# One activation table, k normalised before its transpose, and a merged low-rank product in an attention and mixer kernel

## The chip, the cores and the metric

The kernel runs on one core of one Trainium2 chip. The core's engines are TensorE (PE; its weight loads are listed apart as PEld), VectorE (DVE), ScalarE (ACT), GpSimd (POOL) and SyncE (SP). Each takes its own instructions strictly in order of its queue, and semaphores hold an instruction until what it needs is done. The metric is the device time of one launch in microseconds.

## The reference

Eight batches, each with twelve heads of 448 rows and 64 columns. First cosine attention: q and k are divided by their norms, the scores divided by tau = 0.1, then softmax, then the product with v. The heads' outputs side by side form `x` of 448 x 768 per batch. Then a mixer: a low-rank mix along the sequence, added to `x`, and a two-layer network along the channels with a residual.

```python
q_n = q / (norm(q) + 1e-06);  k_n = k / (norm(k) + 1e-06)
attn = softmax(q_n @ k_n.T / tau)
x = heads_side_by_side(attn @ v)              # (8, 448, 768)
u = x + (x.T @ U @ V).T                       # U (448, 32), V (32, 448)
out = u + relu(u @ w_ch1) @ w_ch2             # w_ch1 (768, 3072), w_ch2 (3072, 768)
```

## The kernel before, in words

The sequence of 448 is cut into four parts of 112 rows (row = 4 s + c, for c = 0 to 3), which lie on 112 partitions. Heads are taken two at a time: a batch has six pairs, 48 pairs in all. Everything is computed in bf16 with fp32 sums in PSUM.

`attention_pair` (from L92) does one pair. POOL issues six DMAs (L101, L105, L109: two each for q, k and v, with a cast from fp32 to bf16 on the way) and then writes a column of ones behind v (L112), from which the sums of the softmax come. The three tiles come from pools with six buffers, so the q load of pair n has to wait until pair n-6 is done with its q, and likewise for k and v. DVE squares q and k and sums each row (L118 to L121, eight sums each). ScalarE then takes `Ln` of the sixteen sums (L124) and computes the inverse norms as `Exp(-0.5 * ln)`, once for q with ln(1/tau) as the bias (L125) and once for k (L127). DVE multiplies q by its inverse norm (L131). TensorE transposes q and k in eight small matmuls against the identity (L138, L143); DVE copies q's transpose out (`qT`, L149) and k's twice, each time with one head's rows masked to zero (`kTz`, L151, L153). For each head and each of four parts of k, TensorE makes 112 x 448 scores (L160) and ScalarE takes their exponential (L166); k's inverse norm comes in there, as a scale operand with one value per partition. With the exponentials as weights, TensorE makes `av_ps` in 16 matmuls per head (L178), and DVE divides by the sums (L185, L187) into `X_sb`. No maximum is subtracted.

The mixer of a batch runs while the attention of the next batch runs, in seven pieces. Piece 0 starts with `moe_stage0` (L190): TensorE transposes `X_sb` (L199, 24 matmuls) and DVE copies it out (L204); TensorE makes A = U^T x in eight matmuls of 384 columns (L210) and ScalarE copies it out (L216); TensorE makes h from A and V in six matmuls of 448 columns (L221), and DVE adds h and the transposed x into `uT_all` (L227). Pieces 0 to 3 are the first layer, `moe_mlp1`: 24 groups of six matmuls (L235), each ending in a relu on ScalarE (L241). Pieces 4 and 5 are the second layer, `moe_mlp2`: six groups of 24 matmuls (L248), each ending in an add on DVE (L254). The last piece, `moe_store`, transposes the result back (L264), copies it out on ScalarE (L270) and stores it through SP's queue. After the last batch's attention its mixer runs alone.

The weights of the two layers come in 30 DMAs (L89), issued by POOL among the first batch's loads. The order of each engine's queue is not the order of the text: a scheduler of the framework orders the instructions by costs that it assumes, and puts in the semaphores. In what it made, ScalarE takes the `Ln` of pair n after the exponentials of pair n-6 (from pair 13 on), and in the first batch just after those of pair n-1. It also puts in the loads of ScalarE's function table where the next function isn't in the table that is loaded.

The PSUM tags are `ps_tp` (all transposes, two buffers), `ps_sc` (scores, two), `ps_av` (two) and `ps_mlp` (stage 0 and both layers, two).

Of the kernel before, what the change touches and what calls it, by code (L numbers as in the profile page):

```python
# [9 lines left out]
FP = mybir.dt.float32  # L10
# [6 lines left out]
def kernel(  # L17
# [26 lines left out]
    ln_inv_tau = math.log(inv_tau)  # L44
# [6 lines left out]

    ident = const.tile([128, 128], BF, name="ident")
    make_identity(nc, ident)

    b_lt = const.tile([128, 1], FP, name="b_lt")
    nc.gpsimd.memset(b_lt, ln_inv_tau)
# [14 lines left out]

    V_sb = const.tile([128, SCH, SC], BF, name="V_sb")
    nc.gpsimd.memset(V_sb, 0.0)
    nc.gpsimd.dma_start(out=V_sb[0:R], in_=moe_V.rearrange("r (s c) -> r s c", c=SC))

# [6 lines left out]
    for nch in range(NC):  # L82
        weight_dmas.append((w2_sb[:, nch, :], moe_w_ch2[nch * 128:(nch + 1) * 128, :]))
# [7 lines left out]
    emit_weight_dmas.done = 0  # L91

    def attention_pair(b, p, X_sb):
# [14 lines left out]
        for hh in range(2):  # L108
# [15 lines left out]
        nc.scalar.activation(lnq2, q2k2, AF.Ln)  # L124
        nc.scalar.activation(inv_qk[:, :, :, 0], lnq2[:, :, :, 0], AF.Exp,  # L125
                             bias=b_lt[0:SCH, :], scale=-0.5)
        nc.scalar.activation(inv_qk[:, :, :, 1], lnq2[:, :, :, 1], AF.Exp,  # L127
                             bias=b_zero[0:SCH, :], scale=-0.5)

        qn_pair = attnp.tile([SCH, SC, 2, D], BF, name="qn_pair", tag="qn_pair")  # L130
        nc.vector.tensor_mul(  # L131
            qn_pair, q_pair,
            inv_qk[:, :, :, 0:1].to_broadcast([SCH, SC, 2, D]))
# [3 lines left out]
        for c in range(SC):  # L137
            nc.tensor.transpose(  # L138
                out=qkT_ps[:, c, :],
                in_=qn_pair[:, c, :, :],  # L140
                identity=ident[:SCH, :SCH],
            )
            nc.tensor.transpose(  # L143
                out=qkT_ps[:, SC + c, :],
                in_=k_pair[:, c, :, :],
                identity=ident[:SCH, :SCH],
            )
# [9 lines left out]
        for hh in range(2):  # L157
            for jc in range(SC):
                sc_ps = psum.tile([SCH, S], FP, name="sc_ps", tag="ps_sc", bufs=2)
                nc.tensor.matmul(  # L160
                    out=sc_ps,
                    lhsT=kTz[:, hh, jc, :],
                    rhs=qT.rearrange("p a b -> p (a b)"),
                    start=True, stop=True,
                )
                nc.scalar.activation(  # L166
                    out=attn_uT[:, hh, jc, :],
                    in_=sc_ps,
                    func=AF.Exp,
                    scale=inv_qk[:, jc, hh, 1:2],  # L170
                )

        for hh in range(2):
# [18 lines left out]
    def moe_stage0(b, X_sb):  # L192

        XT_all = batchp.tile([128, CC, S], BF, name="XT_all", tag="XT_all")
        for cc in range(CC):
            xt_ps = psum.tile([128, SC, SCH], BF, name="xt_ps", tag="ps_tp",
                              bufs=2)
            for sb in range(SC):
                nc.tensor.transpose(  # L199
                    out=xt_ps[:, sb, :],  # L200
                    in_=X_sb[:, sb, cc * 128:(cc + 1) * 128],
                    identity=ident[:SCH, :SCH],
                )
            nc.vector.tensor_copy(out=XT_all[:, cc, :], in_=xt_ps)  # L204

        A_sb = batchp.tile([128, 2, C // 2], BF, name="A_sb", tag="A_sb", bufs=1)
        for half in range(2):
            a_ps = psum.tile([128, 512], FP, name="a_ps", tag="ps_mlp", bufs=2)
            for sb in range(SC):
                nc.tensor.matmul(  # L210
                    out=a_ps[:, 0:C // 2],
                    lhsT=U_sb[:, sb, :],
                    rhs=X_sb[:, sb, half * (C // 2):(half + 1) * (C // 2)],
                    start=(sb == 0), stop=(sb == SC - 1),
                )
            nc.scalar.copy(out=A_sb[:, half, :], in_=a_ps[:, 0:C // 2])  # L216

        uT_all = batchp.tile([128, CC, S], BF, name="uT_all", tag="uT_all")
        for cc in range(CC):
            h_ps = psum.tile([128, S], FP, name="h_ps", tag="ps_mlp", bufs=2)  # L220
            nc.tensor.matmul(  # L221
                out=h_ps,
                lhsT=A_sb.rearrange("p a b -> p (a b)")[:, cc * 128:(cc + 1) * 128],
                rhs=V_sb.rearrange("r s c -> r c s"),
                start=True, stop=True,
            )
            nc.vector.tensor_add(out=uT_all[:, cc, :], in0=h_ps,  # L227
                                 in1=XT_all[:, cc, :])
        return uT_all

    def moe_mlp1(uT_all, relu1, nchs):
        for nch in nchs:
            m1_ps = psum.tile([128, S], FP, name="m1_ps", tag="ps_mlp", bufs=2)
            for cc in range(CC):
                nc.tensor.matmul(  # L235
                    out=m1_ps,
                    lhsT=w1_sb[:, cc, nch * 128:(nch + 1) * 128],
# [3 lines left out]
            nc.scalar.activation(out=relu1[:, nch, :], in_=m1_ps, func=AF.Relu)  # L241

    def moe_mlp2(uT_all, relu1, ccs):
        outT = uT_all
        for cc in ccs:
            m2_ps = psum.tile([128, S], FP, name="m2_ps", tag="ps_mlp", bufs=2)
            for nch in range(NC):
                nc.tensor.matmul(  # L248
                    out=m2_ps,
                    lhsT=w2_sb[:, nch, cc * 128:(cc + 1) * 128],  # L250
                    rhs=relu1[:, nch, :],
                    start=(nch == 0), stop=(nch == NC - 1),
                )
# [21 lines left out]
    def _split(n, k):  # L275
        base, rem = divmod(n, k)
        res, start = [], 0
        for i in range(k):
# [74 lines left out]
```

## Time and profile before

| what | value |
|---|---|
| median of 5 runs | 818.09 us (817.6 to 819.26) |
| the profiled execution | 822.62 us, of which its span is 820.8 |
| granted TensorE clock, mean | 0.989 |
| PE busy | 717.7 us (87%), 5104 matmuls |
| ACT busy | 494.8 us (60%) |
| DVE busy | 307.1 us (37%) |
| POOL busy | 226.6 us (28%) |
| q, k and v loads: time to issue, and median from issue to landing | 0.70 us each; 2.8, 2.8 and 2.9 us |

A group in the profile is one line's instructions on one engine: its busy time, the mean of one in nanoseconds, then how long the engine was idle just before such an instruction and what ended the wait. The end of a matmul is modelled and matmuls overlap, so PE's busy time says little of how fully it is used; the distance between the starts of matmuls that follow each other says more. The chain is found by going back from the last instruction, at each step to what released it. "issue" is time in which an engine waited for nothing that the profile shows.

### The profile page before, as it was taken

Reading aid. Unit: us, or ns where it says so; the run is one execution under the profiler, and the core shown is the slowest. Engines: PE = TensorE matmul, PEld = TensorE weight load, DVE = VectorE, ACT = ScalarE, POOL = GpSimd, SP = SyncE. Lnnn points to the kernel's source line nnn. Section 1 sums busy time; section 2 is a strip of 40 time slices with the busy share of each in tenths; the row PEclk is TensorE's granted clock in tenths of the full one; section 3 lists DMA queues with packets and bytes.
Section 4 is the critical chain, followed back from the end, with each engine's and each line's share of the span. In section 5 each row is a group of like instructions: output and inputs, shape, how many; then the busy total and the mean of one; then the engine's idle time right before and its main releaser. Section 6 shows DMA issues by size and latency. Waiting matters only on the chain.

```text
span 820.8 us, 12706 instructions
## 1 busy us (share of the span) xinstructions
PE 717.7 (87%) x5104; PEld 427.2 (52%) x5104; DVE 307.1 (37%) x720; ACT 494.8 (60%) x862; POOL 226.6 (28%) x382
## 2 busy tenths in 40 slices
PE   3456777999889989899979998899979999999996
PEld 2344544555455555556545555455545556654553
DVE  2253673434433362444424362344523351123000
ACT  3467688944785478844777369755778357622411
POOL 6477932321323232221423231422322100000000
PEclk9999999999999999999999999999999999999999
DMA  8999952524524262424524261434342120002002
GB/s 122 188 140 144 76 37 18 36 18 85 34 18 30 22 91 20 27 19 85 34 18 29 18 97 12 31 21 86 24 29 18 12 68 1 2 1 68 1 0 68
DMA packets 142618, 37.84 MB, mean 46 GB/s; under 512 B 135104, under 2 KB 138208, under 8 KB 142560
## 3 DMA queue, kind: packets, MB, share of 16 engines
q0 software_dynamic: 138464, 26.03, 38.6%
q1 hardware_dynamic: 4096, 11.01, 4.2%
q8 instruction: 40, 0.66, 0.3%
q14 instruction: 18, 0.15, 0.1%
HBM read 52.02 MB, written 11.01 MB: 77 GB/s over the span
## 4 chain that ended last, share of the span: by engine, by line
PE 62%; ACT 18%; issue 7%; DMA 6%; DVE 3%; POOL 3%; DVEq 0%; POOLq 0%; ACTq 0%
PE m_ps L248 25%; PE m_ps L235 16%; PE sc_ps L160 9%; PE av_ps L178 6%; ACT L124 4%; ACT attn_uT L166 4%; ACT L166 3%; DMA q_pair<-in_q_dram 3%; ACT relu L241 3%; DMA v_pair<-in_v_dram 2%; PE o_ps L264 1%; PE h_ps L221 1%; PE a_ps L210 1%; ACT O_sb L270 1%; POOL v_pair L109 1%
## 5 line engine op out<-in xcount | busy, mean ns | idle before, releaser
L166 ACT ACTIVATE attn_uT<-sc_ps,inv_qk 112x448 bf16<-112x448 f32 x384 | 221.2, 633 | 105.2 <-PE sc_ps L160 101.9
L235 PE MATMUL m_ps<-uT_all,w_sb 128*128 128x448 bf16 x1152 | 251.7, 357 | 10.3 <-ACT relu L241 9.7
L248 PE MATMUL m_ps<-relu,w_sb 128*128 128x448 bf16 x1152 | 234.6, 352 | 0.0
L160 PE MATMUL sc_ps<-qT,kTz 128*112 128x448 bf16 x384 | 141.9, 391 | 43.1 <-ACT attn_uT L166 26.2
L178 PEld LDWEIGHTS <-attn_uT 112*112 112x112 bf16 x1536 | 124.9, 141 | 81.2 <-issue 32.2
L235 PEld LDWEIGHTS <-w_sb 128*128 128x128 bf16 x1152 | 107.3, 99 | 106.4 <-issue 24.3
L248 PEld LDWEIGHTS <-w_sb 128*128 128x128 bf16 x1152 | 107.7, 98 | 91.6
L241 ACT ACTIVATE relu<-m_ps 128x448 bf16<-128x448 f32 x192 | 101.0, 539 | 89.4 <-PE m_ps L235 89.3
L178 PE MATMUL av_ps<-v_pair,attn_uT 112*112 112x65 bf16 x1536 | 145.4, 221 | 3.2 <-ACT attn_uT L166 3.2
L109 POOL DMA_DIRECT2D v_pair<-in_v_dram x96 | 67.1, 703 | 272.6 <-issue 263.5
L105 POOL DMA_DIRECT2D k_pair<-in_k_dram x96 | 67.0, 703 | 98.6 <-PE qkT_ps L143 83.8
L270 ACT CAST O_sb<-o_ps 112x768 f32<-112x768 bf16 x32 | 23.2, 808 | 100.4 <-PE o_ps L264 100.4
L160 PEld LDWEIGHTS <-kTz 128*112 128x112 bf16 x384 | 52.5, 143 | 44.0 <-DVE kTz L151 26.5
L254 DVE TENSOR_TENSOR uT_all<-m_ps,uT_all 128x448 bf16<-128x448 f32 x48 | 29.9, 623 | 120.5 <-PE m_ps L248 120.5
L101 POOL DMA_DIRECT2D q_pair<-in_q_dram x96 | 67.3, 706 | 8.5 <-DVE qn_pair L131 3.5
L118 DVE TENSOR_TENSOR sq_tmp<-q_pair 112x512 bf16<-112x512 bf16 x48 | 20.3, 423 | 114.3 <-DMA q_pair<-in_q_dram 114.1
L185 DVE RECIPROCAL rd<-av_ps 112x4 f32<-112x4 f32 x96 | 17.2, 179 | 119.3 <-PE av_ps L178 118.9
L124 ACT ACT_TABLE_LOAD x47 | 60.3, 1283 | 1.8 <-PEq L334 0.7
L138 PE MATMUL qkT_ps<-ident,qn_pair 112*128 112x112 bf16 x192 | 27.6, 225 | 37.0 <-DVE qn_pair L131 35.8
L131 DVE TENSOR_TENSOR qn_pair<-q_pair,inv_qk 112x512 bf16<-112x512 bf16 x48 | 33.1, 689 | 43.3 <-ACT inv_qk L125 43.2
L166 ACT ACT_TABLE_LOAD x37 | 47.5, 1283 | 0.7
L187 DVE TENSOR_TENSOR X_sb<-av_ps,rd 112x256 bf16<-112x256 f32 x96 | 40.6, 423 | 2.6
(42 smaller groups left out, 457.5 us busy)
## 6 DMA issues: line engine op xcount, KB each, us to landing
out_dram<-O_sb SPq DMA_DIRECT2D x32, 336.0 KB, 3.6
q_pair<-in_q_dram POOLq DMA_DIRECT2D x96, 56.0 KB, 2.8
k_pair<-in_k_dram POOLq DMA_DIRECT2D x96, 56.0 KB, 2.8
v_pair<-in_v_dram POOLq DMA_DIRECT2D x96, 56.0 KB, 2.9
w_sb<-in_moe_w_ch_dram POOLq DMA_DIRECT2D x6, 768.0 KB, 8.6
w_sb<-in_moe_w_ch_dram POOLq DMA_DIRECT2D x24, 192.0 KB, 6.0
U_sb<-in_moe_U_dram POOLq DMA_DIRECT2D x1, 28.0 KB, 2.5
V_sb<-in_moe_V_dram POOLq DMA_DIRECT2D x1, 28.0 KB, 2.6
```

The source lines that it names most:

```text
L101: nc.gpsimd.dma_start(out=q_pair[:, :, hh, :], in_=q[b, h0 + hh].rearrange("(s c) d -> s c d", c=SC))
L105: nc.gpsimd.dma_start(out=k_pair[:, :, hh, :], in_=k[b, h0 + hh].rearrange("(s c) d -> s c d", c=SC))
L109: nc.gpsimd.dma_start(out=v_pair[:, :, hh, 0:D], in_=v[b, h0 + hh].rearrange("(s c) d -> s c d", c=SC))
L124: nc.scalar.activation(lnq2, q2k2, AF.Ln)
L131: nc.vector.tensor_mul(qn_pair, q_pair, inv_qk[:, :, :, 0:1].to_broadcast([SCH, SC, 2, D]))
L160: nc.tensor.matmul(out=sc_ps, lhsT=kTz[:, hh, jc, :], rhs=qT.rearrange("p a b -> p (a b)"), start=True, stop=True,)
L166: nc.scalar.activation(out=attn_uT[:, hh, jc, :], in_=sc_ps, func=AF.Exp, scale=inv_qk[:, jc, hh, 1:2],)
L178: nc.tensor.matmul(out=av_ps[:, ic, 0:D + 1], lhsT=attn_uT[:, hh, jc, ic * SCH:(ic + 1) * SCH], rhs=v_pair[:, jc, hh, :], start=(jc == 0), ...
L187: nc.vector.tensor_mul(X_sb[:, :, c0:c0 + D], av_ps[:, :, 0:D], rd.to_broadcast([SCH, SC, D]))
L235: nc.tensor.matmul(out=m1_ps, lhsT=w1_sb[:, cc, nch * 128:(nch + 1) * 128], rhs=uT_all[:, cc, :], start=(cc == 0), stop=(cc == CC - 1),)
L241: nc.scalar.activation(out=relu1[:, nch, :], in_=m1_ps, func=AF.Relu)
L248: nc.tensor.matmul(out=m2_ps, lhsT=w2_sb[:, nch, cc * 128:(cc + 1) * 128], rhs=relu1[:, nch, :], start=(nch == 0), stop=(nch == NC - 1),)
```

## The change

Five things change.

1. The table set `natural_log_exp_and_others` is loaded once, ahead of everything else.
2. k is multiplied by its inverse norm on DVE before its transpose (`kn_pair`), and 1/tau goes into the product for q (`scalar_tensor_tensor`). One `Exp` on ScalarE gives both inverse norms, and the exponentials of the scores have no scale operand.
3. The matrix M = I + U V is computed once at the start, in bf16 (`M_sb`), from a transposed U and an identity whose columns are in V's order (`ident_int`). Stage 0 is then x^T M in one step: for each of the six parts of the channels, four matmuls of 448 columns into `u_ps`, and one DVE copy. The transposes of x, A, and h are gone.
4. The `Ln` of pair n is tied to come, in ScalarE's order, after the last exponential of an earlier pair: pair n-1 up to n = 6, then a distance that grows to five pairs. The tie is one of order on the same engine and has no semaphore.
5. Names of loop variables change (`nch` to `ncb`, `k` to `parts`).

The scheduler orders all queues anew.

```diff
-    ln_inv_tau = math.log(inv_tau)
...
+    nc.scalar.preload_act_table_set("natural_log_exp_and_others")
     ident = const.tile([128, 128], BF, name="ident")
     make_identity(nc, ident)
-    b_lt = const.tile([128, 1], FP, name="b_lt")
-    nc.gpsimd.memset(b_lt, ln_inv_tau)
...
+    ident_int = const.tile([SCH, SC, S], BF, name="ident_int")
+    nc.gpsimd.memset(ident_int, 0.0)
+    for cs in range(SC):
+        make_identity(nc, ident_int[:, cs, cs * SCH:(cs + 1) * SCH], nomemset=True)
+
+    uT_ps = psum.tile([128, SC, SCH], BF, name="uT_ps", tag="ps_tp", bufs=2)
+    for cs in range(SC):
+        nc.tensor.transpose(
+            out=uT_ps[:, cs, :],
+            in_=U_sb[:, cs, :],
+            identity=ident[:SCH, :SCH],
+        )
+    U_T = const.tile([128, SC, SCH], BF, name="U_T")
+    nc.vector.tensor_copy(out=U_T, in_=uT_ps)
+
+    M_sb = const.tile([SCH, SC, S], BF, name="M_sb")
+    for cs in range(SC):
+        m_ps = psum.tile([SCH, S], FP, name="m_ps", tag="ps_mlp", bufs=2)
+        nc.tensor.matmul(
+            out=m_ps,
+            lhsT=U_T[:, cs, :],
+            rhs=V_sb.rearrange("r s c -> r c s"),
+            start=True, stop=True,
+        )
+        nc.vector.tensor_add(out=M_sb[:, cs, :], in0=m_ps,
+                             in1=ident_int[:, cs, :])
...
+    last_exp = {}
...
-        nc.scalar.activation(lnq2, q2k2, AF.Ln)
-        nc.scalar.activation(inv_qk[:, :, :, 0], lnq2[:, :, :, 0], AF.Exp,
-                             bias=b_lt[0:SCH, :], scale=-0.5)
-        nc.scalar.activation(inv_qk[:, :, :, 1], lnq2[:, :, :, 1], AF.Exp,
+        ln_i = nc.scalar.activation(lnq2, q2k2, AF.Ln)
+        n = b * NPAIR + p
+        if n > 0:
+            gate = n - 1 if n <= 6 else max(6 + (n - 7) // 2, n - 5)
+            tc.add_manual_dep(
+                ln_i.ins, last_exp[gate].name,
+                mybir.DependencyInfo(mybir.DependencyClass.NoSync,
+                                     mybir.DependencyReason.DATA),
+                reason="Ln after the last exponential of an earlier pair")
+        nc.scalar.activation(inv_qk, lnq2, AF.Exp,
                              bias=b_zero[0:SCH, :], scale=-0.5)
...
+        nc.vector.scalar_tensor_tensor(
+            out=qn_pair, in0=q_pair, scalar=inv_tau,
+            in1=inv_qk[:, :, :, 0:1].to_broadcast([SCH, SC, 2, D]),
+            op0=ALU.mult, op1=ALU.mult)
+        kn_pair = attnp.tile([SCH, SC, 2, D], BF, name="kn_pair", tag="kn_pair")
         nc.vector.tensor_mul(
-            qn_pair, q_pair,
-            inv_qk[:, :, :, 0:1].to_broadcast([SCH, SC, 2, D]))
+            kn_pair, k_pair,
+            inv_qk[:, :, :, 1:2].to_broadcast([SCH, SC, 2, D]))
...
-                in_=k_pair[:, c, :, :],
+                in_=kn_pair[:, c, :, :],
...
-                nc.scalar.activation(
+                e_i = nc.scalar.activation(
                     out=attn_uT[:, hh, jc, :],
                     in_=sc_ps,
                     func=AF.Exp,
-                    scale=inv_qk[:, jc, hh, 1:2],
-                )
-
+                )
+
+        last_exp[n] = e_i.ins
...
     def moe_stage0(b, X_sb):
...
         uT_all = batchp.tile([128, CC, S], BF, name="uT_all", tag="uT_all")
         for cc in range(CC):
+            u_ps = psum.tile([128, S], FP, name="u_ps", tag="ps_mlp", bufs=2)
+            for cs in range(SC):
+                nc.tensor.matmul(
+                    out=u_ps,
+                    lhsT=X_sb[:, cs, cc * 128:(cc + 1) * 128],
+                    rhs=M_sb[:, cs, :],
+                    start=(cs == 0), stop=(cs == SC - 1),
+                )
+            nc.vector.tensor_copy(out=uT_all[:, cc, :], in_=u_ps)
         return uT_all
```

## The prediction

> **What bounds the kernel now.** I read the page's busy shares first, then the groups by line, then a table of stretches cut where the first mlp1 matmul of each batch starts (105.46, 204.93, 297.02 ... 755.47), and last the chain and ScalarE's timeline inside one stretch.
>
> The groups (busy, mean ns of one, then the idle time before them):
>
> ```profile
> L166 ACT ACTIVATE attn_uT<-sc_ps,inv_qk 112x448 bf16<-112x448 f32 x384 | 221.2, 633 | 105.2 <-PE sc_ps L160 101.9
> ...
> L241 ACT ACTIVATE relu<-m_ps 128x448 bf16<-128x448 f32 x192 | 101.0, 539 | 89.4 <-PE m_ps L235 89.3
> ...
> L124 ACT ACT_TABLE_LOAD x47 | 60.3, 1283 | 1.8 <-PEq L334 0.7
> ...
> L131 DVE TENSOR_TENSOR qn_pair<-q_pair,inv_qk 112x512 bf16<-112x512 bf16 x48 | 33.1, 689 | 43.3 <-ACT inv_qk L125 43.2
> L166 ACT ACT_TABLE_LOAD x37 | 47.5, 1283 | 0.7
> ```
>
> With ten more loads at L125, ScalarE reloads its table 94 times, 120.6 us, because Ln and Exp alternate. Is that on the path? The stretches (us, busy PE, PEld, DVE, ACT, POOL, granted clock, DMA share, GB/s):
>
> ```profile
> 0.00:105.46 105.46, 58.43 (x382) 41.89 (x383) 44.27 (x106) 60.21 (x99) 75.19 (x136) 1.00 1.18 132
> 105.46:204.93 99.47, 88.34 (x647) 51.89 (x647) 46.98 (x109) 71.17 (x122) 28.07 (x46) 0.98 0.41 38
> ...
> 485.33:578.30 92.97, 85.75 (x640) 50.99 (x638) 38.66 (x91) 61.58 (x108) 25.92 (x43) 1.00 0.40 38
> ...
> 673.01:755.47 82.46, 80.94 (x575) 46.88 (x573) 22.33 (x58) 39.09 (x74) 0.00 (x0) 1.00 0.06 18
> 755.47:820.80 65.33, 58.17 (x312) 30.27 (x311) 4.23 (x7) 15.98 (x28) 0.00 (x0) 0.94 0.07 22
> ```
>
> The last full stretch (673 on) has no loads and no DMA from POOL: PE idles 1.5 us in it, in a middle batch 7.2. But it holds one attention pair less (575 records against 640), so 82.5 is no target yet. The chain inside the middle batch says what stops PE (start, us, what):
>
> ```profile
> 489.34 1.28 ACT L124
> ...
> 493.23 1.28 ACT L166
> ...
> 500.32 1.28 ACT L124
> ...
> 504.74 8.35 issue
> ...
> 514.49 0.69 POOL q_pair L101
> 515.18 3.61 DMA q_pair<-in_q_dram
> 518.88 0.44 DVE sq_tmp L118
> ...
> 520.81 0.58 PE sc_ps L160 x2
> ...
> 527.04 1.28 ACT L124
> ...
> 530.93 1.28 ACT L166
> ...
> 570.30 1.28 ACT L166
> ```
>
> Two causes: loads that hold back a relu or the first exponential; and a q load that POOL issues only after the v load ahead of it (which waits for an old pair's av), while DVE's in-order queue has this q's square ahead of the present pair's qT and kTz. Otherwise PE is the bound.
>
> PE's own work in one batch, from start-to-start times: mlp1 and mlp2 288 x 0.189 (55 in 10.41 us) = 54.4; scores 48 x 0.189 = 9.1; av 192 x 0.058 (13 in 0.76) = 11.2; q/k transposes 48 x 0.05 = 2.4; output transposes 24 x 0.053 = 1.3; stage 0: X transposes 24 x 0.05 = 1.2, A 8 x 0.163 = 1.3, h 6 x 0.19 = 1.15. Sum 82.1 of 92.97: 10.9 us of gaps.
>
> **The change, part by part.**
> *Table set preloaded.* The instruction order that both programs are built to shows 94 loads before and one after, at the start. ScalarE loses 93 x 1.283 = 119.3 us. The Trainium skill ("ScalarE: Activation LUTs", What ACT_TABLE_LOAD costs) prices each switch at 1283 ns plus a 1380 ns drain, 2.66 us; that would make 247 us. ScalarE's timeline (start, us, operation) has no drain between the load and what follows:
>
> ```profile
> 77.98 1.28 ACT L124 ACT_TABLE_LOAD   x1
> 79.27 0.21 ACT L124 ACTIVATE lnq<-q2k 112x16 f32<-112x16 f32 x1
> 79.50 1.28 ACT L125 ACT_TABLE_LOAD   x1
> ```
>
> So I take the row, 1.28. In a middle batch the loads (two a pair) are worth only what they keep PE waiting, and that lies in the 10.9 us of gaps; in the first batch, where each pair waits for the one before, the two of a pair lie on the path whole: 2.57 us.
>
> *Exponentials without a scale operand.* L166 takes 633 ns, the relu of the same length, without pointer operands, 539. The trace can't say whether the 94 ns are Exp's or the operand's; the same section of that page gives each pointer operand about 93 ns and every function the same rate. I take 540: 384 x 0.093 = 36 us of ScalarE. If the page did not hold here it is 0. In a middle batch a pair's eight exponentials take 4.56 us (7 x 0.56 + 0.63); consecutive scores share two PSUM buffers, so the pitch falls by about half of the 93 ns: 4.15. This matters because the new PE order puts fewer mlp matmuls among the scores (m2 pairs: 9 where there were 12; m1: 8 to 11 where there were 11 to 15). Work from the first score to the last av group in an m2 pair: 8 x 0.189 + 9 x 0.189 + 19 x 0.058 = 4.3, against 0.5 + 4.15 = 4.65 of ScalarE: 0.3 to 0.4 idle a pair, as now (5.1 against 4.9). At 633 ns it would be 0.8.
>
> *k normalised on DVE.* One more 112x512 product, nearest row L131, 0.69: 33 us of DVE, which is 37% busy. The qn product becomes a two-operator form with no row: between L118's 0.42 and two passes of L131, 1.38; I take 0.69, as the fp32 broadcast is the same. In the steady state both stand three pairs ahead of use and cost nothing; in the first batch, where pair waits for pair, kn adds its 0.6 pitch. The two small Exps (0.30 + 0.19 pitch) become one.
>
> *Stage 0.* PE loses 3.65 (above) and gains 24 x 0.189 = 4.54: +0.9. ScalarE loses the A copies (7.2 us in all), DVE six XT copies at 0.385 per batch; six adds become six copies, 0.62. The boundary loses its serial path (A copy, then h paced by DVE's adds at 0.61): PE's stretch from o_ps to mlp1 was 284.15 to 296.84, 12.7 us. Now work there is 1.3 + 4.5 + 3.4 (one pair) + 1.2 = 10.4, and 0.5 to 1 idle while O_sb copies (4 x 0.73) free the transposes' buffer.
>
> *Ln gate and order.* In the new order Ln of pair n stands after the exponentials of pair n-5 (before, n-6), and its Exp right behind it; q's square stands ahead of the present pair's reciprocal rather than ahead of the next pair's qT. But POOL's queue now has the ones-memset (which waits for v's landing) ahead of the q issue. Counted from an av's end: v issues 1.4, lands 2.6, q issues 1.4, lands 2.8, so the square can go at +8.3; the reciprocal behind it is wanted at about +8.4. PE needs nothing from it until the next pair's qT, two pairs on. I price this at 0; uncovered it is the third rival.
>
> *Preparing M.* Ahead of the first q issue POOL gets a memset of 1792 columns (535 ns for 512: 1.9) and four selects (0.29 each): +3.1 us, and all DMA with it. PE's queue opens with U's four transposes and four matmuls, DVE's with a copy and four adds (0.62 each) that wait for V: behind them stands pair 0 alone, whose first square goes at about 11.6, not 7.46. Pairs 1 and 2 wait for DMA anyway, so of these 4 us only the 3.1 of the DMA remain.
>
> **The sum**, by stretch.
> *Until the first mlp1 matmul, 105.5 now.* Pairs 0 to 2 are timed by DMA (the square of pair 1 waits until 27.2): +3.1. From pair 2 on the period is 12.2 (exponentials end at 53.5, 65.8, 78.0, 90.1). New: Ln and Exp 0.6, qn to kTz to score 3.85 + 0.6, exponentials 5.2: about 10. But DVE's new order has the square of pair 5 ahead of pair 3's reciprocals and of pair 7 ahead of pair 5's qT; q7 was issued at 76.9, is now at 80, lands at 83.5. So pair 5 ends near 91, and pair 6 needs q9 (94). Ln to kn 2, transposes and kTz 2, the last u copy: first mlp1 matmul at 97. The shorter period alone, with no wait for these loads, would put it at about 90.
> *First batch with mlp, 99.5.* POOL runs at 4.7 us a pair to catch up and the squares of pairs 12, 14 and 16 hold DVE; about 7 us of stalls: 92.
> *Five middle batches, 468.1.* 82.1 + 0.9 = 82.9 work, 5 x 0.35 idle, 0.5 in the boundary: 85 each, 425.
> *Last full one, 82.5.* Its work is 82.9 less one pair (8 x 0.189 + 32 x 0.058 + 24 x 0.05 = 4.6), 78.3; idle 2.2 (1.5 as now, and the wait for the last u copy): 80.5. By the same count the present one has 77.5 of work and 5 of gaps, 4.1 of them in its stage 0. *Tail,* unchanged, 65.3.
> Together 97 + 92 + 425 + 80.5 + 65.3 = 759.8 of span. The profiled execution took 822.62 for a span of 820.8, and the median of the runs is 818.09, 2.7 under the span: **757 us**.
>
> **Rivals.**
> *A, PE tight from the start (15%).* POOL's early waits shrink as the pairs get faster: first matmul at 90, then 86, 5 x 83.3, 79, 65: 737, median 734. For it: POOL's waits between 40 and 70 us are short (0.3 to 0.8). Against: the DMA share of that stretch is 1.18.
> *B, ScalarE still paces the pairs (12%).* Exp stays at 633: 0.5 more for 42 pairs, 21 us: 778. For it: no Exp without the operand in the trace.
> *C, the square holds DVE (15%).* Landing of q reaches 4.6 at the most after 200 us; 1 us over on each of some 24 m1 pairs: 781.
> *D, slower (3%).* The same queue closes into a loop: av end, v 4.0, q 4.2, square and reduction 1.1, then reciprocals, kTz, scores and av of the pair after next, about 9: 18.5 us in two pairs, which PE needs 21 for. It decides above 21; to lose all of 61 us over 28 m1 pairs, 2.2 us each, both landings would have to be near 6: 830.
> *E, not as it says (1%).* Loads could return or the set be left out: 818. The built order has one load.
>
> **How the numbers follow.** The first forecast has 54%, with its own range of 745 to 769. 735 to 781 leaves out half of A and half of C, D and E, some 2 in 10. Within 0.2% of 818.09 (1.6 us; about what these runs can tell from no change) is only E, 1%; faster 96%, slower 3%.
>
> **What would show it.** One load row; L166's successor near 540; PE's idle in a middle batch near 2 to 3; no chain piece of a q load before a score; the first mlp1 matmul near 97; batches of 85. Wrong if the reciprocals wait for squares, if exponentials stay at 633, or if u_ps waits for DVE's copies.

## The result and the profile after

The median is 753.78 us (752.04 to 755.15) against 818.74 us for the kernel before in the same comparison: a ratio of 0.9205, 95% interval 0.9192 to 0.9218. One of the nine executions was slow, 765.33 us with a granted clock of 0.952, and stands outside this range and the ratio. The forecast was 757, its own range 745 to 769. The profiled execution took 753.76 us, its span is 751.9 us.

The page of the kernel after: busy shares, the chain's shares by engine, and three groups (busy, mean ns of one, idle before and what ended it).

```profile
PE 705.9 (94%) x5000; PEld 420.2 (56%) x5000; DVE 316.5 (42%) x725; ACT 331.7 (44%) x705; POOL 229.4 (31%) x386
...
PE 87%; DMA 7%; POOL 3%; ACT 1%; issue 1%; DVE 1%; POOLq 0%; DVEq 0%; ACTq 0%
...
L203 ACT ACTIVATE attn_uT<-sc_ps 112x448 bf16<-112x448 f32 x384 | 191.7, 544 | 160.2 <-PE sc_ps L197 157.2
...
L253 ACT ACTIVATE relu<-m_ps 128x448 bf16<-128x448 f32 x192 | 104.2, 543 | 115.3 <-PE m_ps L247 115.3
```

The exponentials now take what a relu takes, 544 ns. ScalarE fell from 494.8 to 331.7 us, and nearly all its waits are waits for TensorE. 87% of the chain is PE. Two groups of the full list of the same kernel: one table load is left of 94, and the new product for k takes 682 ns, with DVE never idle before it (the 0.0).

```profile
L168 DVE TENSOR_TENSOR kn_pair<-k_pair,inv_qk 112x512 bf16<-112x512 bf16 x48 | 32.7, 682 | 0.0
...
L51 ACT ACT_TABLE_LOAD x1 | 1.3, 1283 | 0.7 <-PEq L346 0.7
```

The table of stretches of the kernel after, cut as before at the first mlp1 matmul of each batch: the start, the first batch with a mixer, one middle batch, the last full one, the tail (us, busy PE, PEld, DVE, ACT, POOL, granted clock, DMA share, GB/s).

```profile
0.00:95.91 95.91, 57.70 (x329) 37.13 (x330) 44.44 (x103) 28.96 (x63) 68.29 (x125) 0.85 1.17 137
95.91:186.26 90.35, 89.80 (x676) 54.07 (x675) 55.65 (x127) 46.21 (x106) 43.28 (x69) 0.99 0.66 55
270.65:355.03 84.38, 84.32 (x625) 50.52 (x624) 39.30 (x91) 41.14 (x88) 25.36 (x42) 1.00 0.43 41
608.26:688.49 80.23, 80.22 (x567) 46.69 (x566) 20.04 (x49) 34.81 (x68) 0.00 (x0) 1.00 0.05 15
688.49:751.90 63.41, 56.51 (x313) 29.77 (x311) 4.38 (x7) 15.98 (x28) 0.00 (x0) 0.96 0.08 26
```

In a middle batch PE is busy 84.32 of 84.38 us. Its chain holds no q load and no table load; the only piece of another engine is one exponential of 0.55 us. From one pair to the next there is nothing between but TensorE's own work (start, us, what).

```profile
305.31 0.70 PE av_ps L215 x13
306.01 3.22 PE m_ps L247 x17
309.62 1.51 PE m_ps L260 x8
311.13 0.47 PE sc_ps L197 x2
311.60 0.57 PE m_ps L260 x3
```

Where the 68.9 us of span came from (us, this table and the one of before):

| stretch | before | forecast | after | gain |
|---|---|---|---|---|
| until the first mlp1 matmul | 105.5 | 97 | 95.9 | 9.6 |
| first batch with a mixer | 99.5 | 92 | 90.4 | 9.1 |
| five middle batches | 468.1 | 425 | 422.0 | 46.1 |
| last full batch | 82.5 | 80.5 | 80.2 | 2.2 |
| tail | 65.3 | 65.3 | 63.4 | 1.9 |

The first two rows hold different work before and after. The old order makes the scores of seven pairs ahead of the first mlp1 matmul, the new one those of six, so the stretch behind it has seven pairs where it had six. The scores in that stretch (8 matmuls a pair), before and after:

```profile
L160 PE MATMUL sc_ps<-qT,kTz 128*112 128x448 bf16 x48 | 16.9, 372 | 5.7 <-ACT attn_uT L166 5.3 <-DVE kTz L151 0.3
...
L197 PE MATMUL sc_ps<-qT,kTz 128*112 128x448 bf16 x56 | 19.1, 362 | 0.5 <-ACT attn_uT L203 0.4
```

So only the sum of the two rows, 18.7 us, compares like with like.

### The profile page after: what moved, and what is told of

Read it like the earlier page. It is cut to its first block, busy times and chain, and to the rows that moved or that the text cites. A ratio compares the mean times of both kernels' runs of the same rounds, so it can differ in the third digit from the quotient of the medians.

```text
span 751.9 us, 12268 instructions
## 1 busy us (share of the span) xinstructions
PE 705.9 (94%) x5000; PEld 420.2 (56%) x5000; DVE 316.5 (42%) x725; ACT 331.7 (44%) x705; POOL 229.4 (31%) x386
## 4 chain that ended last, share of the span: by engine, by line
PE 87%; DMA 7%; POOL 3%; ACT 1%; issue 1%; DVE 1%; POOLq 0%; DVEq 0%; ACTq 0%
PE m_ps L247 29%; PE m_ps L260 29%; PE sc_ps L197 11%; PE av_ps L215 9%; PE u_ps L234 5%; DMA v_pair<-in_v_dram 4%; DMA w_sb<-in_moe_w_ch_dram 3%; PE o_ps L276 2%; PE qkT_ps L180 1%; PE qkT_ps L175 1%; POOL q_pair L127 1%; POOL k_pair L131 1%; ACT attn_uT L203 1%; POOL v_pair L135 1%; DMA q_pair<-in_q_dram 0%
## 5 line engine op out<-in xcount | busy, mean ns | idle before, releaser
L203 ACT ACTIVATE attn_uT<-sc_ps 112x448 bf16<-112x448 f32 x384 | 191.7, 544 | 160.2 <-PE sc_ps L197 157.2
L247 PE MATMUL m_ps<-uT_all,w_sb 128*128 128x448 bf16 x1152 | 248.9, 353 | 0.0
L260 PEld LDWEIGHTS <-w_sb 128*128 128x128 bf16 x1152 | 110.8, 98 | 93.8
L247 PEld LDWEIGHTS <-w_sb 128*128 128x128 bf16 x1152 | 109.6, 99 | 87.4 <-issue 0.9
L253 ACT ACTIVATE relu<-m_ps 128x448 bf16<-128x448 f32 x192 | 104.2, 543 | 115.3 <-PE m_ps L247 115.3
L215 PE MATMUL av_ps<-v_pair,attn_uT 112*112 112x65 bf16 x1536 | 143.6, 220 | 1.8 <-ACT attn_uT L203 1.8
L197 PE MATMUL sc_ps<-qT,kTz 128*112 128x448 bf16 x384 | 137.9, 383 | 7.2 <-DVE kTz L188 4.2
L197 PEld LDWEIGHTS <-kTz 128*112 128x112 bf16 x384 | 50.4, 140 | 25.6 <-DVE kTz L188 15.6
L222 DVE RECIPROCAL rd<-av_ps 112x4 f32<-112x4 f32 x96 | 17.4, 181 | 103.0 <-PE av_ps L215 99.7
L234 PE MATMUL u_ps<-M_sb,X_sb 112*128 112x448 bf16 x192 | 53.4, 380 | 2.0 <-DVE X_sb L224 1.8
L163 DVE SCALAR_TENSOR_TENSOR qn_pair<-q_pair,inv_qk 112x512 bf16<-112x512 bf16 x48 | 32.9, 684 | 42.9 <-PE qkT_ps L180 41.3
L175 PE MATMUL qkT_ps<-ident,qn_pair 112*128 112x112 bf16 x192 | 28.1, 224 | 19.3 <-DVE qn_pair L163 19.3
L240 DVE CAST uT_all<-u_ps 128x448 bf16<-128x448 f32 x48 | 29.3, 621 | 17.8 <-PE u_ps L234 16.9
```

What stands on the lines that cost most here:

```text
L175: nc.tensor.transpose(out=qkT_ps[:, c, :], in_=qn_pair[:, c, :, :], identity=ident[:SCH, :SCH],)
L197: nc.tensor.matmul(out=sc_ps, lhsT=kTz[:, hh, jc, :], rhs=qT.rearrange("p a b -> p (a b)"), start=True, stop=True,)
L203: e_i = nc.scalar.activation(out=attn_uT[:, hh, jc, :], in_=sc_ps, func=AF.Exp,)
L215: nc.tensor.matmul(out=av_ps[:, ic, 0:D + 1], lhsT=attn_uT[:, hh, jc, ic * SCH:(ic + 1) * SCH], rhs=v_pair[:, jc, hh, :], start=(jc == 0), ...
L234: nc.tensor.matmul(out=u_ps, lhsT=X_sb[:, cs, cc * 128:(cc + 1) * 128], rhs=M_sb[:, cs, :], start=(cs == 0), stop=(cs == SC - 1),)
L247: nc.tensor.matmul(out=m1_ps, lhsT=w1_sb[:, cc, ncb * 128:(ncb + 1) * 128], rhs=uT_all[:, cc, :], start=(cc == 0), stop=(cc == CC - 1),)
```

## The experiments

Theory: the batches are TensorE's own work once ScalarE's loads, the late pair inputs and stage 0's serial path no longer hold it; the start is timed by POOL's queue. Most runs below undo or add one part. Times are medians with the range of the runs; times of stretches are those of the one profiled execution of a run. The kernel before had medians between 816.95 and 820.89 us beside them, so parts are compared by ratio; a difference of ratios times 818.74 gives us.

**The loads put back, all else new.**

```diff
-    nc.scalar.preload_act_table_set("natural_log_exp_and_others")
```

> The kernel after with the one table load at the start taken out again, so that the table is switched before almost every Ln and after it (90 loads); ScalarE's queue is otherwise in the same order. Theory 1 (the loads were on the path: they hold back the relus and exponentials that PE waits for): 90 x 1.28 us more on ScalarE, of which some 6 to 7 us per batch reach PE in the mlp1 slots; middle batches 90 to 91 us instead of 84.4, total about 795 to 805 us. Rival (once k is normalised ahead and ScalarE is only 44% busy, loads are covered by idle time, and the gain came from the new order): middle batches 84 to 86, total 754 to 765 us.

790.81 us (790.29 to 791.05), ratio 0.9649 [0.9634, 0.9663]: 0.0444 or 36.4 us more than with one load. A middle batch is 88.8 us (4.4 more, less than expected), the first one with a mixer 102.7 (12.3 more). The group of mlp1 matmuls shows the way: 23.9 us of waits for a relu, of which the kernel after has none in that row.

```profile
L246 PE MATMUL m_ps<-uT_all,w_sb 128*128 128x448 bf16 x1152 | 257.0, 355 | 25.5 <-ACT relu L252 23.9
```

ScalarE's timeline in the same run, inside a middle batch (start, us, operation):

```profile
404.30 1.28 ACT L149 ACT_TABLE_LOAD   x1
405.59 0.22 ACT L149 ACTIVATE lnq<-q2k 112x16 f32<-112x16 f32 x1
405.71 0.53 ACT L252 ACTIVATE relu<-m_ps 128x448 bf16<-128x448 f32 x1
406.25 1.28 ACT L158 ACT_TABLE_LOAD   x1
407.55 0.31 ACT L158 ACTIVATE inv_qk<-lnq,b_zero 112x16 f32<-112x16 f32 x1
```

One relu gets between two loads, and the mlp1 buffers (two) are then full. Ln starts 1.29 us after its load, so the load costs 1.28 and no drain on top: the row that the prediction took, and not the 2.66 of the Trainium skill ("ScalarE: Activation LUTs", What ACT_TABLE_LOAD costs).

**The loads taken out, all else old.** One line in the kernel before; its instruction order is the same but for the loads.

```diff
+    nc.scalar.preload_act_table_set("natural_log_exp_and_others")
```

> The kernel before with the one table load at the start and nothing else; all queues keep their order, the 94 loads become one. Theory 1 (loads are the larger of the two causes of PE's 10.9 us of gaps per batch): middle batches fall from 93.6 to about 87, first mlp1 matmul from 105.5 to about 96, total about 770 to 778 us. Rival (the q load that DVE waits for takes the place of the loads, since it is in the chain of every batch): middle batches 90 to 92, total 795 to 808 us.

781.78 us (780.37 to 783.68), ratio 0.9541 [0.9522, 0.9559]: 37.6 us, about what the run before shows from the other side, and less than the theory wanted. Middle batches are 87.6 to 89.7 us (92.1 to 95.0 before). PE still waits for kTz, which DVE makes behind the square of a q that has not landed. In one such place DVE stands 5.3 us for a q whose square starts at 484.77 us; the transposes that it has to copy next are done at 482.8, their copy starts at 485.90, and PE waits 2.5 us for it. All such waits of PE (us in total, times, longest):

```profile
PE sc_ps L161 <- DVE kTz L152: 21.0, 12, 3.0
```

In the kernel after this wait is 4.2 us in all.

**A scale operand of ones on the exponentials of the new kernel.** It settles whether the old 633 ns were Exp or the operand, and whether they cost time.

```diff
+    s_one = const.tile([128, 1], FP, name="s_one")
+    nc.gpsimd.memset(s_one, 1.0)
...
                     func=AF.Exp,
+                    scale=s_one[0:SCH, :],
```

> The kernel after with a scale operand of ones (one value per partition) on the exponentials of the scores; the result is the same numbers. The scheduler puts more mlp matmuls among the scores again. Theory (the pointer operand costs the 90 ns, not the function): exponentials at 633 to 637 ns instead of 544; middle batches 85 to 87, total 757 to 770 us. Rival a (the function Exp cost it and something else made it faster): exponentials stay near 544, total 752 to 755. Rival b (the longer exponentials are covered by PE's fillers): 633 ns, but middle batches still at 84.4 to 85, total 752 to 757 us.

755.45 us (753.11 to 757.07), ratio 0.9208 [0.9189, 0.9228], where 0.9205 is without the operand: no difference that these intervals can tell; rival b held. The operand is what costs, 632 against 544 ns:

```profile
L205 ACT ACTIVATE attn_uT<-sc_ps,s_one 112x448 bf16<-112x448 f32 x384 | 220.9, 632 | 154.0 <-PE sc_ps L199 150.4
```

So the Trainium skill ("ScalarE: Activation LUTs", What ACT_TABLE_LOAD costs: about 93 ns for each pointer operand) agrees with 88 ns measured. But a middle batch is 84.5 us, 0.1 more. The order of PE changed with the assumed cost: among the scores of the six pairs of a batch stand 11, 10, 10, 8, 8 and 5 matmuls of the mixer, where the kernel after has 9, 8, 8, 6, 6 and 3. That these two more a pair cover the longer exponentials is an inference; the operand with PE's order held fixed was not run.

**The old stage 0 in the new kernel** (transposes of x, A, h; no M).

```diff
-    ident_int = const.tile([SCH, SC, S], BF, name="ident_int")
...
-        nc.vector.tensor_add(out=M_sb[:, cs, :], in0=m_ps,
-                             in1=ident_int[:, cs, :])
...
     def moe_stage0(b, X_sb):
...
-                    lhsT=X_sb[:, cs, cc * 128:(cc + 1) * 128],
-                    rhs=M_sb[:, cs, :],
...
-            nc.vector.tensor_copy(out=uT_all[:, cc, :], in_=u_ps)
+            nc.vector.tensor_copy(out=XT_all[:, cc, :], in_=xt_ps)
...
+            nc.scalar.copy(out=A_sb[:, half, :], in_=a_ps[:, 0:C // 2])
...
+            nc.vector.tensor_add(out=uT_all[:, cc, :], in0=h_ps,
+                                 in1=XT_all[:, cc, :])
```

> The kernel after with stage 0 as before (transposes of x, A, h and the add, and no M). Theory: PE has 0.9 us less work per batch, but the serial path through the A copy and DVE's adds is back: middle batches 86 to 87 instead of 84.4, the last full one about 2.6 us longer, the first mlp1 matmul some 3 us earlier for the shorter preparation and some 3 later for stage 0's own path: total 762 to 772 us. Rival (stage 0's path is covered by attention's matmuls, and less PE work wins): 744 to 752 us.

772.27 us (771.71 to 774.7), ratio 0.9429 [0.9411, 0.9447]: 18.3 us. The profiled execution (774.7 us) was the slowest of the four; in it the old form costs 6.8 in the start (102.7) and takes 0.9 less in the next stretch, which again holds six pairs and not seven, so 5.9 in the two; then 2.2 in each middle batch (86.6), 2.3 in the last full one and 1.7 in the tail. The 5.9 were not in what was expected, which let the start's two terms of 3 us cancel. The six parts of u each need only one pair's heads, so the new form runs while the attention of the first batch runs. The copies of u in the kernel after, until the first mlp1 matmul (durations min, median, max in ns; first and last start):

```profile
L240 DVE CAST uT_all<-u_ps x5: 614/615/625, 30.8 to 86.1; 128x448 bf16<-128x448 f32 x5
```

Five of six lie before 87 us. The old form takes A in halves of three pairs; in this run the second half's matmuls come at 92.77 us, after the sixth pair, and all six h behind them, from 94.4 to 102.2.

The tail's 1.7 us are a matter of TensorE's clock. The same table of stretches around the first mlp1 matmul of the last batch, in pieces of 2 us, first in the kernel before (mlp1 starts at 755.47):

```profile
751.47:753.47 2.00, 1.57 (x16) 0.91 (x14) 2.00 (x6) 0.00 (x0) 0.00 (x0) 1.00 0.96 327
753.47:755.47 2.00, 1.55 (x3) 0.20 (x3) 1.89 (x5) 0.00 (x0) 0.00 (x0) 1.00 0.10 34
755.47:757.47 2.00, 2.00 (x6) 0.86 (x6) 0.48 (x1) 0.00 (x0) 0.00 (x0) 0.50 0.00 0
757.47:759.47 2.00, 2.00 (x9) 0.86 (x7) 0.00 (x0) 0.54 (x1) 0.00 (x0) 0.65 0.00 0
```

and in the kernel after (688.49):

```profile
686.49:688.49 2.00, 2.00 (x12) 0.95 (x11) 1.56 (x3) 0.00 (x0) 0.00 (x0) 1.00 0.99 323
688.49:690.49 2.00, 2.00 (x12) 1.07 (x11) 0.62 (x1) 0.54 (x1) 0.00 (x0) 1.00 0.33 123
```

Before, h is paced by DVE's adds (busy 1.89 to 2.00 of 2), with three matmuls in the last 2 us; then the granted clock is 0.50 and mlp1 gets 6 matmuls done in 2 us where the kernel after gets 12. A window of 4 us from there holds 13 matmuls against 23, which at 0.189 us each is 1.9 us. All four kernels with the old stage 0 (before, the two with only the loads or also the tie added to it, and this one) have a granted clock of 0.58 to 0.63 there and a tail of 64.9 to 65.3 us; all ten with the new one have 1.00 and 63.4 to 63.9. The Trainium skill ("TensorE: Matmul & The Clock Gate", What's actually happening) has the gate fall to half after an idle window of about 3.4 us; here the longest single wait of PE that the trace lists in the 9 us ahead of it was 0.43 us, and PE was busy 4.57 of the last 6, so no such window stood ahead of the fall. That the sparse work brought it is what the comparison of the kernels suggests.

**No tie between Ln and an earlier pair's exponentials.**

```diff
-        if n > 0:
-            gate = n - 1 if n <= 6 else max(6 + (n - 7) // 2, n - 5)
-            tc.add_manual_dep(
-                ln_i.ins, last_exp[gate].name,
...
```

> The kernel after without the tie that puts Ln after an earlier pair's last exponential; the scheduler places Ln by its own costs (earlier, from pair 5 on). Theory (the tie is priced at nothing: Ln is never what PE waits for once pairs run ahead): total 748 to 758 us. Rival (without the tie ScalarE's queue stands at a Ln whose q and k have not landed, and exponentials wait behind it): first two stretches 10 to 20 us longer, total 765 to 775 us.

766.72 us (762.51 to 768.35), ratio 0.9327 [0.9286, 0.9368]: 10.0 us more (the interval leaves some 3 either way), so the theory, which priced the tie at nothing, fell. The rival had the total right, but not the place: it put 10 to 20 us into the first two stretches, which are 1.9 longer (the start 3.3 shorter, the first batch with a mixer 95.5), while the five middle batches, 85.8 to 87.8 us each, lose 12.2 in all. ScalarE's waits, in the run without the tie:

```profile
ACT lnq L150 <- DVE q2k L147: 72.1, 26, 10.7
ACT lnq L150 <- DVE rd L215: 19.9, 13, 2.4
```

and in the kernel after:

```profile
ACT lnq L150 <- DVE q2k L147: 24.1, 3, 10.8
```

Left alone, the scheduler puts Ln early in ScalarE's queue, where it stands and waits for sums of inputs that have not landed. Behind it stand relus, and PE waits for them; in the kernel after it has no such wait.

```profile
PE m_ps L240 <- ACT relu L246: 8.6, 11, 2.0
```

One such place in the chain of the run without the tie (start, us, what):

```profile
471.09 4.30 DMA k_pair<-in_k_dram
475.49 0.44 DVE sq_tmp L146
475.95 0.69 DVE q2k L147
476.74 0.21 ACT lnq L150
476.95 0.44 ACT relu L246
477.43 1.29 PE m_ps L240 x6
```

A k load, its square, its sums, then Ln, and only then the relu that mlp1 waits for. With the tie Ln waits 3 times instead of 39.

**The tie, and no loads, in the kernel before.** Does the tie alone do it?

```diff
+    nc.scalar.preload_act_table_set("natural_log_exp_and_others")
...
-        nc.scalar.activation(lnq2, q2k2, AF.Ln)
+        ln_i = nc.scalar.activation(lnq2, q2k2, AF.Ln)
+        n = b * NPAIR + p
+        if n > 0:
+            gate = n - 1 if n <= 6 else max(6 + (n - 7) // 2, n - 5)
+            tc.add_manual_dep(
+                ln_i.ins, last_exp[gate].name,
...
```

> The kernel before with the one table load at the start and with the tie of Ln to an earlier pair's last exponential; q, k, the exponentials and stage 0 as before. Theory (with the loads out, what is left between e2's 88.7 and e4's 86.6 us of a middle batch is the square of q that stands ahead of the next pair's qT in DVE's queue while its load is late, and the tie's new order removes it): middle batches 86.4 to 87.0, total 770 to 777 us. Rival (it takes k's product on DVE as well, which frees POOL's k loads from TensorE's transposes): middle batches 88 to 89, total 778 to 784 us.

779.02 us (775.07 to 779.48), ratio 0.9514 [0.9482, 0.9546]: 2.2 us better than without the tie, and the intervals overlap, so the tie alone is not seen to do anything; the rival held. Middle batches are 87.2 to 89.6 us. PE's wait for kTz stays:

```profile
PE sc_ps L171 <- DVE kTz L162: 18.2, 12, 2.5
```

From here to the new kernel with the old stage 0 (0.9429) only k's product on DVE, the single Exp and the missing scale operand are added: 0.0085, 7.0 us, and PE's wait for kTz falls to 5.6. POOL's k loads no longer stand until TensorE has transposed an earlier k (POOL's group, here and with the old stage 0 in the new kernel; the idle time before it is the last number):

```profile
L108 POOL DMA_DIRECT2D k_pair<-in_k_dram x96 | 67.0, 703 | 97.3 <-PE qkT_ps L154 81.0
```

```profile
L104 POOL DMA_DIRECT2D k_pair<-in_k_dram x96 | 66.9, 702 | 6.8 <-DVE XT_all L214 3.3
```

That this is what gains the 7.0 us (k's buffer comes free by a DVE product, not by a transpose in TensorE's queue) is inferred; k's product was not tried alone.

**The start: weights spread over two batches; the column of ones ahead of v's loads; M prepared after the second pair.**

```diff
-    def emit_weight_dmas(frac):
-        upto = int(len(weight_dmas) * frac)
+    def emit_weight_dmas(upto):
...
             if b == 0:
-                emit_weight_dmas((p + 1) / (NPAIR + 1.0))
+                emit_weight_dmas(min(p + 1, CC))
+            elif b == 1:
+                emit_weight_dmas(CC + min(p + 1, 4) * NC // 4)
```

> The kernel after with the weight loads moved: the six of the first layer one by one behind each of the first six pairs, the 24 of the second layer behind pairs 6 to 9. Theory (until the first mlp1 matmul the pairs are timed by loads that queue behind weights, as priced: 97 instead of 90): first mlp1 matmul at 84 to 90 instead of 95.9, the next stretch 90 to 95, total 742 to 750 us. Rival (the serial chain of a pair, not the loads, sets this stretch; or the second layer's weights come late): first matmul at 94 to 96 or the second stretch longer by as much, total 752 to 762 us.

```diff
+        nc.gpsimd.memset(v_pair[:, :, :, D:D + 1], 1.0)
         for hh in range(2):
...
                 in_=v[b, h0 + hh].rearrange("(s c) d -> s c d", c=SC))
-        nc.gpsimd.memset(v_pair[:, :, :, D:D + 1], 1.0)
```

> The kernel after with the ones column of v written ahead of v's loads instead of behind them, so that POOL's queue no longer stands at v's landing (2.6 us) before the next q load. All other queues keep their order. Theory (that wait was priced at 0 in the middle batches, as the square is two pairs from the qT that PE needs): middle batches stay at 84.4 within 0.2; the stretch of the first mlp batch may shorten by up to 2; total 749 to 754 us. Rival (the square holds DVE's queue and PE feels it): middle batches 83.0 to 83.8, total 742 to 748 us.

```diff
...
+    def make_m():
+        ident_int = const.tile([SCH, SC, S], BF, name="ident_int")
...
+            if b == 0 and p == 1:
+                make_m()
```

> The kernel after with M prepared after pair 1's loads are issued, so that the first q load is again issued at 3.6 us. Theory (the preparation delays every load of the first stretch by 3.1 us): first mlp1 matmul at about 93 instead of 95.9, total about 749 to 751 us. Rival (the delay is taken up by POOL's later waits): 95 to 96, total 752 to 754 us.

By the medians each is small, 4.9, 2.1 and 2.5 us: 748.93 us (747.55 to 750.87; ratio 0.9113 [0.9079, 0.9146]), 751.71 (751.56 to 753.09; 0.9156 [0.9128, 0.9184]) and 751.29 (750.84 to 751.4; 0.9146 [0.9119, 0.9173]). In all three a middle batch is 84.38 us, as without them: POOL's memset that waits for v (80.8 us in all) costs the middle batches nothing, as the prediction had it. With the weights spread the first mlp1 matmul comes at 85.0, 10.9 sooner, and 7.9 of it is lost in the next stretch. The three together, and the first two together:

> The kernel after with the weight loads spread as in e6, the ones ahead of v's loads as in e7, and M prepared later as in e8. Theory (POOL's queue has a fixed amount to issue up to about pair 12, and moving it only shifts where PE waits; e7 and e8 take time off that queue, 2.4 and 2.5 us, e6 gave 2.8): first two stretches together 178 to 181 instead of 186.3, total 744 to 747 us. Rival (the three overlap, and each takes away the same wait): 182 to 183.5, total 748 to 749.5 us.

> e11 without the later preparation of M: the weight loads spread and the ones written ahead of v's loads. e11 gained 17 us more than after, where its three moves alone gave 2.8, 2.4 and 2.5. Theory (the ones that stand behind v's landing, which in turn queues behind weights, hold POOL's queue, so that the spread alone cannot bring the loads forward; the two moves need each other): first two stretches together 168 to 172 instead of e11's 166.7 and after's 186.3, total 736 to 740 us. Rival (it is the early first load that lets the spread work): 178 to 182, total 745 to 749 us.

| | until the first mlp1 | next | both | median us | ratio [95%] |
|---|---|---|---|---|---|
| after | 95.9 | 90.4 | 186.3 | 753.78 | 0.9205 [0.9192, 0.9218] |
| spread | 85.0 | 98.2 | 183.3 | 748.93 | 0.9113 [0.9079, 0.9146] |
| ones | 93.9 | 90.0 | 183.9 | 751.71 | 0.9156 [0.9128, 0.9184] |
| M later | 92.6 | 91.2 | 183.8 | 751.29 | 0.9146 [0.9119, 0.9173] |
| spread, ones | 84.2 | 90.0 | 174.2 | 741.81 | 0.9044 [0.9017, 0.9070] |
| all three | 72.3 | 94.4 | 166.7 | 734.53 (733.47 to 735.9) | 0.8982 [0.8958, 0.9006] |

With all three the kernel is faster than both, before and after, and by more than theory or rival expected (178 to 181 and 182 to 183.5 for the two stretches together). The run without the later M lies between its theory and its rival. In the first two stretches the three are worth 19.6 us together and 3.0, 2.4 and 2.5 apart; by the medians it is 19.3 against 4.9, 2.1 and 2.5. The ratios say otherwise: 18.3 us together against 7.5, 4.0 and 4.8, hardly more than their sum of 16.3, because the kernel before took 820.89 us beside the single moves and 816.95 beside the three. In favour of the plain times is that a middle batch takes 84.4 us in all of these runs. But the kernel after was not run beside them, so it is likely, and not settled, that the moves need each other. POOL's lines show what they could share. Its timeline with the weights spread (start, us, operation, idle before):

```profile
13.93 0.14 POOL L137 MEMSET v_pair<- 112x8 bf16 x1 [2.67 <-DMA v_pair<-in_v_dram]
14.17 1.40 POOL L126 DMA_DIRECT2D q_pair<-in_q_dram  x2
...
21.57 0.14 POOL L137 MEMSET v_pair<- 112x8 bf16 x1 [2.69 <-DMA v_pair<-in_v_dram]
21.81 1.40 POOL L126 DMA_DIRECT2D q_pair<-in_q_dram  x2
```

In the kernel after:

```profile
31.54 0.14 POOL L138 MEMSET v_pair<- 112x8 bf16 x1 [5.43 <-DMA v_pair<-in_v_dram]
...
33.37 1.43 POOL L127 DMA_DIRECT2D q_pair<-in_q_dram  x2
```

With all three moves:

```profile
8.83 1.40 POOL L128 DMA_DIRECT2D q_pair<-in_q_dram  x2
...
21.97 1.40 POOL L128 DMA_DIRECT2D q_pair<-in_q_dram  x2 [1.16 <-DMA w_sb<-in_moe_w_ch_dram]
```

A memset of 0.14 us waits for v to land and holds all loads behind it: 5.4 us at the worst in the kernel after, and 2.0 to 3.8 at each of the first six pairs with the weights spread. In the kernel after the queue also stands 10 us for weights until 42 us. The third pair after the first is asked for at 44.7 us in the kernel after, at 28.7 with the weights spread and at 24.5 with the ones moved as well. The loss after the first mlp1 matmul with the weights spread is the same queue: 8 us of it that start 12 us after that matmul, and below them the same 8 us with the ones moved too (columns as above).

```profile
97.03:105.03 8.00, 2.52 (x12) 1.06 (x10) 4.50 (x10) 1.08 (x4) 7.11 (x12) 0.73 1.32 85
```

```profile
96.16:104.16 8.00, 8.00 (x69) 5.09 (x67) 5.37 (x15) 6.29 (x16) 4.86 (x9) 1.00 0.95 62
```

PE does 2.5 us of work in 8 while POOL, busy 7.1, issues one pair after another; the chain there is POOL's issues, and in this stretch PE waits 6.8 us for two kTz. With the ones moved PE is busy 8 of 8 and has no such wait. M's later preparation saves 2.5 us by itself and 7.5 on top of the other two: 11.9 at the first mlp1 and minus 4.4 in the next stretch. In that stretch PE waits 3.0 us for kTz again; where the 11.9 come from was not settled.

**One load instead of two for each of q, k and v.**

```diff
-        for hh in range(2):
-            nc.gpsimd.dma_start(
-                out=q_pair[:, :, hh, :],
-                in_=q[b, h0 + hh].rearrange("(s c) d -> s c d", c=SC))
+        nc.gpsimd.dma_start(
+            out=q_pair,
+            in_=q[b, h0:h0 + 2].rearrange("h (s c) d -> s c h d", c=SC))
...
```

> The kernel after with one DMA instead of two for each of q, k and v of a pair (both heads in one). Theory (POOL's queue times the first 186 us, and a DMA's issue costs by its descriptors, whose number stays): 1.35 to 1.4 us for one issue, landing 0.3 to 0.7 later, total 750 to 757 us. Rival (issue costs by instruction, 0.7 each): POOL needs 2.1 instead of 4.2 us for a pair, the first two stretches together 176 to 182 instead of 186.3, total 741 to 748 us.

752.57 us (751.98 to 755.27), ratio 0.9208 [0.9176, 0.9241]: no change in time, as the theory said. One issue takes 1.29 us for q, 1.38 for k and 1.32 for v on average (q's median is 1.14) instead of two of 0.70, so POOL saves only 10 us of 202 on them, and its weight issues take 6 more. A q or k lands 4.0 us from the issue, against 3.5 for the second of two (0.70 + 2.8). The first two stretches take 185.4 us against 186.3.

## Why the prediction was right

*The loads.* It took 1.28 us each, 94 of them, and said that in the middle batches they are worth only what they keep PE waiting. Both held: 119 us of ScalarE, 36 to 38 us of time. It gave no number for the loads alone in a middle batch; they are 4.4 to 5 of the 9.2 us. For the first batch it was wrong: "the two of a pair lie on the path whole: 2.57 us" would be some 15 us for six pairs. Taking the loads out of the old kernel made the start 5.8 us shorter (105.5 to 99.7), putting them back into the new one 2.4 longer (95.9 to 98.3).

*The exponentials.* 540 ns forecast, 544 measured. But rival B, which put 21 us on 633 ns, was mis-sized: the run with a scale of ones has the 632 ns and loses nothing that can be told. Its 0.5 us a pair came from a fixed number of matmuls among the scores, and that number is not fixed; the scheduler's order had two more matmuls a pair among the scores there.

*k on DVE.* 0.69 us forecast, 0.682 measured; qn 0.69 against 0.684. "Cost nothing" fits the middle batches, in which PE stands for nothing of it. That the product also frees k's buffer sooner was not foreseen; the 7.0 us above bound it roughly, since the operand and the second Exp are in them.

*Stage 0.* The 0.9 us more of PE work and the shorter boundary gave 85 for a middle batch (84.4; PE's idle time was forecast near 2 to 3 us, and 84.4 is 1.5 above the 82.9 of counted work). Its 18.3 us lie elsewhere too: 5.9 in the first two stretches, where the sum counted only "the last u copy" and never said what the five earlier ones are worth.

*Ln gate and order.* "I price this at 0" held for what it was said of: squares and reciprocals that stand in a new order cost PE nothing. DVE still waits 74.0 us for q, and POOL 80.8 for v, all off the chain in the middle batches. But the 85 came from the order as built, tie included, and 10.0 us of the result hang on it.

*Start and first batch.* 97 against 95.9, 92 against 90.4. The step that POOL's first q issue is 3.1 us later measured 2.9 (3.6 to 6.5 us), and M's preparation costs 2.5 us in all by the medians. The period of "about 10" a pair did not come: the exponentials of pairs 2 to 5 end at 56.4, 65.8, 77.6 and 91.1 us, 11.6 apart on average (12.2 before). The prediction did put the end of pair 5 "near 91", by a q load that holds DVE's queue ahead of pair 5's qT. That is what happened, but with another load: pair 6's q, issued at 71.6, landed at 79.8, and for pair 7's DVE did not wait (the squares of pairs 6 and 7).

```profile
79.92 0.42 DVE L144 TENSOR_TENSOR sq_tmp<-q_pair 112x512 bf16<-112x512 bf16 x1 [7.38 <-DMA q_pair<-in_q_dram]
...
83.25 0.42 DVE L144 TENSOR_TENSOR sq_tmp<-q_pair 112x512 bf16<-112x512 bf16 x1
```

The 92 came near by luck. It was 85 and "about 7 us of stalls", with POOL catching up; the trace lists one wait of PE in that stretch, 0.4 us. What makes it 6 us longer than a middle batch is mostly the seventh attention pair in it, which the sum did not have there.

*Tail.* "Unchanged, 65.3" failed: 63.4. The low clock that follows the old stage 0 is the missing term, 1.7 to 1.9 us.

The parts taken off the new kernel (ratios times 818.74): loads 36.4, stage 0 18.3, tie 10.0, scale operand 0.2, together 64.9 of 65.0 us. That these fill the whole is partly chance: k's product was never taken off alone, and the tie's 10.0 carries some 3 us of noise. Built up from the old one they are loads 37.6, tie 2.2, k's product with the operand and the Exp 7.0, stage 0 18.3; these add up to 65.1 by construction, as each starts where the last one ended. The tie is worth 2 or 10 by what stands beside it, as far as the noise lets one say.

## What to carry to other kernels

Busy time taken off an engine is worth only the waits of the bounding engine that it ends: 119 us of table loads gave 37, 34 us of scale operands gave none once the order had changed with them. In an in-order queue look at what stands behind each instruction that waits for a transfer, however small it is: a logarithm of 0.2 us cost 10 us here, and a memset of 0.14 us held the loads of the start behind v's landing. When parts share a queue, try them together before judging any: three moves that look like 2 to 5 us each by their medians gave 19.3. And before two stretches are compared, count what work each holds.

## What the hardware showed that was not expected

- TensorE's granted clock fell to 0.50 after a stage of sparse matmuls with no single wait over 0.43 us, and the next 4 us had ten matmuls fewer (1.9 us).
- The granted clock was also 0.50 from 75 to 94 us in the kernel after and 1.00 in the kernel before and with the weights spread and the ones moved. An execution of the kernel after with a mean clock of 0.997 took 755.05 us where the profiled one, at 0.976, took 753.76, so it costs nothing that shows. That PE waits for loads there anyway is the likely reason.
- A table load cost 1.28 us with no drain behind it, in the kernel before and with the loads put back.
- A DMA of twice the size (112 KB) took 1.29 to 1.38 us to issue on average where two of 56 KB take 1.41.
